# Newton and word values in PSUM, shorter steps for w_out's row blocks, products of w3 and w_out in set order

## The chip, the cores and the metric

The kernel runs on one NeuronCore of a Trainium2 chip. The metric is the device time in microseconds (us) of one execution; lower is better. Before the change the median of three runs is 1493.96 us.

The engines that matter are TensorE (PE, matrix products into PSUM), VectorE (DVE), ScalarE (ACT), GpSimd (POOL), and SyncE (SP), whose queue issues the DMA transfers here. Each engine works through its own instructions in a fixed order and waits when an operand or a buffer isn't there yet.

## The reference

```python
def _attn_ref(q, k, v, g_norm):                       # 8 batches, 8 heads, 576 rows, 64 columns
    kv = np.einsum('bhsd,bhse->bhde', k, v)
    out = np.einsum('bhsd,bhde->bhse', q, kv)
    rms = np.sqrt(np.mean(out * out, axis=-1, keepdims=True) + 1e-06)
    return (out / rms * g_norm).astype(np.float32)

def _moe_ref(x, w_in, w_out):                         # 4608 x 512, 512 x 2048, 2048 x 512
    h = x @ w_in
    g = h * np.cos(h)
    return (g @ w_out).astype(np.float32)

def _moe2_ref(x, w1, w2, w3, w_out):                  # 512 x 1024 (w1, w2), 1024 x 1024, 1024 x 512
    a = x @ w1
    b = x @ w2
    h = a * b @ w3
    return (h @ w_out).astype(np.float32)
```

The output of each is the x of the next. The weights come as float64, so the kernel gets them as pairs of 32-bit words.

## The kernel before

Products are taken in three passes over pairs of rounded values: each operand is split into hi (an ACT copy, L122) and lo (a subtraction, L124), and `three` (L863 to L866) multiplies hi by hi (L864), hi by lo (L865) and lo by hi (L866).

There are three stages. In the first, up to about 555 us, 144 steps `h_0` to `h_143` each make 128 of the 2048 columns of h for one block of 512 tokens: 12 products of 512 columns in one PSUM bank. After each, ACT and DVE make g from h (L1425, L1426, then the sine at L1399 and the product at L1400, which frees the bank), and for each four such tiles POOL makes four sums (L829 to L832) that are stored with the tiles. In among these steps, by a plan of step numbers (`at(n, where, ...)`, L1368 to L1390), attention goes on for units of 288 rows: `kv` and `out` products, the squares, the inverse root by Newton's method (`emit_newton`, 11 DVE instructions on 128x18 values), and its product with `o` on POOL. Also in among them, weights arrive in chunks of 512 columns of word pairs, whose float32 value DVE makes in four instructions (`Chunk.convert`, L153, L154, L157, L160) after ACT's absolute value at L152. A chunk whose buffer is a `g` or `stage` tile belongs to w_out (u), or comes in the next stage (d, o, a); a chunk of `i` belongs to w_in.

In the second stage, from about 530 to 880 us, g @ w_out is made as seven products of sums of blocks (`part`, tiles X, Y, V, L1027). The sums of w_out (`left_stage`, four groups kk of row blocks, stored by `left_store` and loaded again by `left_pair`) and the first two blocks of g (`load_right`, `split_right`) are made during the last steps of the first stage, from step 122 on. In the third stage w3 @ the second w_out is made first (`emit_wc`, tiles wc and wchl), so that a * b is multiplied by that one matrix; the products are X and V (L1245) and `o`.

PSUM holds eight banks: `acc0` to `acc3` in `ps_acc`, two of `ps_h`, and two of `ps_a` (tag `pa`), which the attention's small products share. A bank is taken again when its last reader is done. DVE's and ACT's instructions and the products stand in the order in which the program was written, but for stretches outside a manual schedule, which a scheduler orders. The DMA queue of SP is one line: a transfer that waits for its buffer or its source holds up all behind it.

## Time and profile before

| | us |
|---|---|
| median of three runs | 1493.96 (1492.59 to 1496.93) |
| the profiled execution | 1492.64 |
| its span | 1490.8 |
| PE busy in the span | 1448.2 (97%) |
| DVE busy | 1002.3 (67%) |
| ACT busy | 695.0 (47%) |
| POOL busy | 630.3 (42%) |
| mean granted clock of TensorE | 0.989 |

The span runs from the first to the last instruction; 1.84 us of the execution lie around it. PE's 42.6 us without work stand in a few places, each named in a table of waits by line and by what released it. [...] In the timeline a bracket gives an instruction's idle time before it and what ended that. Where an instruction of DVE is shown long, it may have stood in the engine without getting on; the time of the same instruction elsewhere tells.

### The profile page before, as it was taken

The page shows a single profiled execution, that of the slowest core. Times are in us where ns is not written, and L with a number is a line of the kernel's source. Part 1 is how long each engine was busy: PE and PEld are TensorE (multiplying, and loading weights), DVE is VectorE, ACT ScalarE, POOL GpSimd, SP SyncE. Part 2 cuts the span into 40 slices and gives each one's busy share as a digit, 9 for nine tenths or more (in the row PEclk, how much of TensorE's full clock was granted, in tenths as well). Part 3 has the DMA queues.
Part 4 walks back from the last instruction along what each step waited for, and adds up shares of the span by engine and source line. Part 5 has one row for each costly group of instructions (what it writes and reads, how often), then busy time and mean ns, then how long its engine had stood idle before and what let it go on. Part 6 is the DMA issues. An engine that isn't in the chain of part 4 may idle for free.

```text
span 1490.8 us, 21208 instructions
## 1 busy us (share of the span) xinstructions
PE 1448.2 (97%) x7632; PEld 1239.4 (83%) x7632; DVE 1002.3 (67%) x1451; ACT 695.0 (47%) x1320; POOL 630.3 (42%) x461
## 2 busy tenths in 40 slices
PE   8999999989989989999999998999999999999998
PEld 6777777777767768998888887999999898999997
DVE  4898876695797768999997338654554555544553
ACT  4656555545545536555555435433443333433331
POOL 0053853676475762222222407543544236444330
PEclk8999999999999989999999999999999999999999
DMA  9265986867777889999999762122220323223312
GB/s 354 92 224 185 327 255 189 280 227 259 235 235 267 277 309 352 376 355 352 367 363 335 243 213 94 43 85 86 71 71 29 114 72 119 92 72 127 128 65 78
DMA packets 146506, 298.75 MB, mean 200 GB/s; under 512 B 16256, under 2 KB 54240, under 8 KB 146400
## 3 DMA queue, kind: packets, MB, share of 16 engines
q1 hardware_dynamic: 145696, 296.80, 57.9%
q8 instruction: 60, 0.98, 0.3%
q10 hardware_dynamic: 704, 0.59, 0.1%
q14 instruction: 46, 0.38, 0.1%
HBM read 184.92 MB, written 112.42 MB: 199 GB/s over the span
## 4 chain that ended last, share of the span: by engine, by line
PE 80%; DVE 9%; DMA 5%; issue 3%; POOL 2%; ACT 1%; SPq 0%; POOLq 0%; DVEq 0%; ACTq 0%
PE X L1245 13%; PE X L1027 12%; PE V L1027 7%; PE V L1245 6%; PE h L864 6%; PE h L865 5%; PE h L866 5%; PE o L865 4%; PE o L864 4%; PE o L866 4%; PE Y L1245 3%; PE Y L1027 3%; PE kv L272 1%; DVE x L124 1%; DVE u L1426 1%
## 5 line engine op out<-in xcount | busy, mean ns | idle before, releaser
L864 PE MATMUL h<-x,w_in 128*128 128x512 f32 x576 | 237.9, 413 | 17.2 <-DVE u L1400 15.0
L1245 PE MATMUL X<-xc,w 128*128 128x384 f32 x1152 | 226.7, 337 | 5.3 <-DVE wchl L124 3.1
L124 POOL TENSOR_TENSOR xc<-x2r,xc 128x768 fp32r<-128x768 f32 x70 | 134.5, 1930 | 228.8 <-ACT xc L122 228.8
L865 PE MATMUL h<-x,w_in 128*128 128x512 f32 x576 | 226.6, 393 | 0.2 <-DVE x L124 0.2
L866 PE MATMUL h<-x,w_in 128*128 128x512 f32 x576 | 226.7, 394 | 0.0
L1245 PEld LDWEIGHTS X<-xc,w 128*128 128x128 f32 x1152 | 204.5, 189 | 13.0 <-DVE wchl L124 3.5
L1027 PE MATMUL X<-g_hl,wl 128*128 128x512 f32 (+1 forms) x960 | 200.2, 368 | 0.0
L1027 PEld LDWEIGHTS X<-g_hl,wl 128*128 128x128 f32 x960 | 167.7, 189 | 30.2
L122 ACT ACTIVATE g_hl<-g_raw 128x1024 fp32r<-128x1024 f32 x126 | 127.2, 1053 | 106.8 <-PE V L1027 31.5
L124 POOL TENSOR_TENSOR g_hl<-g_raw,g_hl 128x1024 fp32r<-128x1024 f32 x31 | 80.1, 2584 | 224.2 <-ACT g_hl L122 177.2
L1426 DVE SCALAR_TENSOR_TENSOR u<-h,r 128x512 f32<-128x512 f32 x136 | 93.2, 685 | 91.3 <-ACT r L1425 70.0
L864 PEld LDWEIGHTS h<-x,w_in 128*128 128x128 f32 x576 | 109.0, 189 | 48.7 <-DVE u L1400 20.1
L124 DVE TENSOR_TENSOR g_hl<-g_raw,g_hl 128x1024 fp32r<-128x1024 f32 x95 | 117.1, 1259 | 44.1 <-ACT g_hl L122 43.9
L1425 ACT ACTIVATE r<-h 128x512 int32<-128x512 f32 x136 | 81.1, 597 | 133.2 <-PE h L866 132.9
L1253 ACT ACTIVATE s<-X 128x384 f32<-128x384 f32 x144 | 66.7, 488 | 152.0 <-PE X L1245 151.9
L866 PEld LDWEIGHTS h<-x,w_in 128*128 128x128 f32 x576 | 109.2, 190 | 23.7
L865 PEld LDWEIGHTS h<-x,w_in 128*128 128x128 f32 x576 | 109.3, 190 | 23.3 <-DVE x L124 1.1
L1245 PE MATMUL V<-xc,w 128*128 128x384 f32 x576 | 116.2, 335 | 0.0
L864 PE MATMUL o<-wchl,ab 128*128 128x512 f32 x288 | 112.3, 391 | 0.7 <-DVE part L1336 0.5
L865 PE MATMUL o<-wchl,ab 128*128 128x512 f32 x288 | 113.0, 392 | 0.0
L866 PE MATMUL o<-wchl,ab 128*128 128x512 f32 x288 | 110.5, 393 | 0.0
L1399 ACT ACTIVATE u<-u 128x512 f32<-128x512 f32 x136 | 85.2, 626 | 48.4 <-DVE u L1426 47.2
(179 smaller groups left out, 2596.3 us busy)
## 6 DMA issues: line engine op xcount, KB each, us to landing
g_raw<-g SPq DMA_DIRECT2D x126, 512.0 KB
x2r<-x_all SPq DMA_DIRECT2D x44, 384.0 KB
kvraw<-in_kv_main_dram SPq DMA_DIRECT2D x32, 512.0 KB
g<-ta SPq DMA_DIRECT2D x32, 512.0 KB
g<-tb SPq DMA_DIRECT2D x32, 512.0 KB
g<-u SPq DMA_DIRECT2D x28, 512.0 KB
g<-u SPq DMA_DIRECT2D x40, 256.0 KB
part<-o SPq DMA_DIRECT2D x36, 256.0 KB
```

The costliest lines, as they stand in the source:

```text
L122: hi = nc.scalar.activation(dst[:, 0], src, AF.Copy)
L124: lo = lo_engine.tensor_tensor(dst[:, 1], src, f32(dst[:, 0]), ALU.subtract)
L272: nc.tensor.matmul(ps[d], k[:, d], v[:, d], start=fresh and i == 0, stop=i == NC, skip_group_check=True,)
L864: nc.tensor.matmul(ps, w[0], x[0], start=first, stop=False)
L865: nc.tensor.matmul(ps, w[0], x[1], start=False, stop=False)
L866: return nc.tensor.matmul(ps, w[1], x[0], start=False, stop=last).ins
L1027: nc.tensor.matmul(ps, w[:, a, i2, ws], g[:, b, q], start=first and half == 0 and q == 0 and n == 0, stop=last and final and q == KH - 1 a ...
L1245: nc.tensor.matmul(ps, w[:, self.i, a, k], x[:, b, k], start=first and k == 0 and n == 0, stop=last and k == 1 and n == 2, skip_group_chec ...
L1253: copied.append(nc.scalar.activation(s, ps, AF.Copy).ins)
L1399: nc.scalar.activation(u, u, AF.Sin, bias=HALF_PI, scale=TWO_PI)
L1425: nc.scalar.activation(r, h_ps[n], AF.Identity, bias=0.25, scale=INV_2PI)
L1426: nc.vector.scalar_tensor_tensor(u, h_ps[n], INV_2PI, r, ALU.mult, ALU.subtract)
```

## The change

Four things change. In `Chunk.convert`, word chunks with a `g` or `stage` buffer make their value in a bank of `ps_a`; the last of the four DVE instructions writes the result to SBUF, as before. In `emit_newton`, the values x and t stand in a bank of `ps_a`; y stays in SBUF. The step `h_8` takes bank `acc2` and `h_9` takes `acc3` in place of the two of `ps_h`, and unit 6 of attention starts at step 15 in place of 14. The row blocks of w_out begin every three steps from 122 in place of every four, one subtraction goes from POOL to DVE, the loads and splits of g's first blocks stand at other steps (each half of a split in a step of its own, the halves of blocks 1 and 3 on DVE in place of POOL), and the first pairs of stored sums are asked for at steps 137 and 138 in place of 142 and 143. The products of `emit_wc` stand in the order in which the program was written.

```diff
@@ -130,6 +130,7 @@
         def __init__(self, name, src, tag, put, again=False):
             self.name, self.src, self.tag, self.put = name, src, tag, put
+            self.home = "psum" if tag in ("g", "stage") else "row"
             self.again = again
         def load(self):
@@ -147,18 +148,23 @@
             lo, hi = self.words[:, :, 0], self.words[:, :, 1]
-            self.f = row(f"{self.name}_f")
-            b = self.f.bitcast(I32)
-            yield nc.scalar.activation(self.f, hi.bitcast(F32), AF.Abs)
-            yield nc.vector.tensor_scalar(self.f, self.f, MOST, LEAST, ALU.min, ALU.max)
+            if self.home == "psum":
+                f = ps_a.tile([P, CHUNK], F32, tag="pa", name=f"{self.name}_ps")
+            else:
+                f = self.f = row(f"{self.name}_f")
+            b = f.bitcast(I32)
+            yield nc.scalar.activation(f, hi.bitcast(F32), AF.Abs)
+            yield nc.vector.tensor_scalar(f, f, MOST, LEAST, ALU.min, ALU.max)
             yield nc.vector.tensor_scalar(
                 b, b, 3, 0x3FFFFFF8, ALU.logical_shift_left, ALU.bitwise_and
             )
             yield nc.vector.scalar_tensor_tensor(
                 b, hi, -0x40000000, b, ALU.bitwise_and, ALU.bitwise_or
             )
+            if self.home == "psum":
+                self.f = row(f"{self.name}_f")
             yield nc.vector.scalar_tensor_tensor(
-                b, lo, 29, b, ALU.logical_shift_right, ALU.bitwise_or
+                self.f.bitcast(I32), lo, 29, b, ALU.logical_shift_right, ALU.bitwise_or
             )
     chunks = []
@@ -329,12 +335,11 @@
     def emit_newton(u):
-        x = rs[u]
-        y, t = (
-            ap.tile([P, RS], F32, tag=f"rs{i}", bufs=2, name=f"rs{i}_{u}") for i in range(2)
-        )
+        at = ps_a.tile([P, 512], F32, tag="pa", name=f"newton_{u}")
+        x, t = (at[:, RS * i:RS * i + RS] for i in range(2))
+        y = ap.tile([P, RS], F32, tag="rs0", bufs=2, name=f"rs0_{u}")
         load["vector"] += 1000
-        nc.vector.tensor_scalar(x, x, EPS, HUGE, ALU.add, ALU.min)
+        nc.vector.tensor_scalar(x, rs[u], EPS, HUGE, ALU.add, ALU.min)
         newton(x, y, t)
         rs[u] = y
@@ -869,10 +874,11 @@
         t, m = steps[n]
         if tag:
             ps = ps_acc.tile([P, 512], F32, tag=tag, name=f"h_{n}")
-        elif n <= HM or n % 4 < 2:
+        elif n < HM or n % 4 < 2 and n > HM + 1:
             ps = ps_h.tile([P, 512], F32, tag="h", name=f"h_{n}")
         else:
-            ps = ps_acc.tile([P, 512], F32, tag=f"acc{n % 4 - 2}", name=f"h_{n}")
+            k = n % 4 - 2 if n > HM + 1 else n - HM + 2
+            ps = ps_acc.tile([P, 512], F32, tag=f"acc{k}", name=f"h_{n}")
         w, x = w_in[m], x_hl[t]
         for c in range(KD):
             h_last[n] = three(
@@ -933,7 +939,7 @@
             (vec if kk < 2 else pool).tensor_tensor(a22, a21, a22, ADD)
             left(0, kk, a11)
         if stage == 1:
-            (pool if kk else vec).tensor_tensor(a21, a11, a21, SUB)
+            (pool if kk > 1 else vec).tensor_tensor(a21, a11, a21, SUB)
             left(1, kk, a12)
         if stage == 2:
             vec.tensor_tensor(a11, a22, a11, SUB)
@@ -993,13 +999,16 @@
             nc.sync.dma_start(out=t, in_=gd[k, 2 * half + r][:, slot])
             raws[i, r] = t
-    def split_right(i):
+    def split_right(i, which=(0, 1)):
         k, p, half, _ = parts_of[i]
         W, KR, KH = shape_of(k)
-        t = x_home((0, 2, 1)[i % 3], [P, 2, KH, W], F32R, f"g_hl_{i}")
-        for r in range(2):
-            split(t[:, :, KR * r:KR * r + KR], raws.pop((i, r)), pool if r and i % 2 else vec)
-        rights[i] = t
+        if i not in rights:
+            rights[i] = x_home((0, 2, 1)[i % 3], [P, 2, KH, W], F32R, f"g_hl_{i}")
+        for r in which:
+            split(
+                rights[i][:, :, KR * r:KR * r + KR], raws.pop((i, r)),
+                pool if r and i % 2 and i > 4 else vec,
+            )
     def part(i):
@@ -1345,7 +1354,7 @@
         }
         end_of = {t: max(n for n, s in enumerate(steps) if s[0] == t) for t in range(NB)}
         ready = plan_first(HM - 1)
-        starts = (14, 22, 29, 36, 44, 52, 59, 78, 86, 93)
+        starts = (15, 22, 29, 36, 44, 52, 59, 78, 86, 93)
         for u, n in zip(range(6, NU), starts):
             ready[u] = plan_unit(u, n, u in (6, 9, 10, 11, 12, 13))
         LIGHT = (*range(48, 54), *range(64, 72), *range(80, 88), *range(98, 104), *range(114, 120))
@@ -1372,20 +1381,20 @@
         for k, n in enumerate(words):
             plan_words(n_first + k, n)
         for kk in range(4):
-            n = 122 + 4 * kk
+            n = 122 + 3 * kk
             at((117, 120, 121, 127)[kk], "end", left_load, kk)
             for k in range(4):
                 at(n + k, "mid", left_stage, kk, k)
-            for l, k in ((3, 2), (5, 3), (6, 5)):
+            for l, k in ((3, 2), (5, 3), (6, 6 if kk == 1 else 5)):
                 at(n + k, "top", left_store, kk, l)
         at(131, "end", load_right, 0)
-        at(135, "end", load_right, 1)
-        at(138, "mid", split_right, 0)
-        at(138, "end", load_right, 2)
-        at(140, "mid", split_right, 1)
-        at(140, "end", load_right, 3)
-        at(NS - 2, "end", left_pair, 0)
-        at(NS - 1, "end", left_pair, 1)
+        at(133, "end", load_right, 1)
+        at(135, "end", load_right, 2)
+        at(139, "end", load_right, 3)
+        for i in range(2):
+            for r in range(2):
+                at(134 + 2 * i + r, "mid", split_right, i, (r,))
+            at(137 + i, "end", left_pair, i)
         for i in range(len(LATE_LEFT)):
             at(NS + i, "mid", left_late, i)
@@ -1523,7 +1532,8 @@
         x0 = xc_early(0, vec)
         next(x0)
         for k, step in enumerate(wc_steps):
-            emit_wc(*step)
+            with tc.manual_schedule(engines={mybir.EngineType.PE}):
+                emit_wc(*step)
             if k + 6 < len(wc_steps):
                 load_w3(k + 6)
             if k + 2 < len(wc_steps):
```

On SP's queue, near the end of the first stage, this stood before. `w_left_3`, `w_left_5` and `w_left_6` are the stored sums of w_out, `g_raw_0` to `g_raw_3` the first four blocks of g for the second stage (two transfers each), `g_4_2` the place in memory of the last tokens' sums, and `w_pair` a pair of stored sums that comes back.

```order
L993 DMA g_raw_1_0_5147<-g_0_2_1592 128x1024
L993 DMA g_raw_1_1_5149<-g_0_3_1737 128x1024
L950 DMA w_left_3_4831<-w_out_13_4948 128x2x256
L950 DMA w_left_5_4861<-w_out_03_4945 128x2x256
L993 DMA g_raw_2_0_5226<-g_0_0_950 128x1024
L993 DMA g_raw_2_1_5228<-g_0_1_1125 128x1024
L950 DMA w_left_6_4919<-w_out_13_4948 128x2x256
L835 DMA g_4_2_5214<-u_7_4_5166 128x2x512
L836 DMA g_4_2_5214<-u_8_4_4968 128x512
L840 DMA g_4_2_5214<-ta_4_4_5215 128x2x512
L840 DMA g_4_2_5214<-tb_4_4_5216 128x2x512
L993 DMA g_raw_3_0_5283<-g_0_2_1592 128x1024
```

And now:

```order
L999 DMA g_raw_1_0_5128<-g_0_2_1584 128x1024
L999 DMA g_raw_1_1_5130<-g_0_3_1736 128x1024
L956 DMA w_left_5_4877<-w_out_03_4963 128x2x256
L999 DMA g_raw_2_0_5179<-g_0_0_950 128x1024
L999 DMA g_raw_2_1_5181<-g_0_1_1119 128x1024
L956 DMA w_left_6_4939<-w_out_13_4966 128x2x256
L972 DMA w_pair_30_5226<-w_left_3_4847 128x1024
L972 DMA w_pair_31_5254<-w_left_3_4847 128x1024
L840 DMA g_4_2_5247<-u_7_4_5198 128x2x512
L841 DMA g_4_2_5247<-u_8_4_4986 128x512
L999 DMA g_raw_3_0_5276<-g_0_2_1584 128x1024
L999 DMA g_raw_3_1_5278<-g_0_3_1736 128x1024
```

The last part of `w_left_3` has moved ahead of `g_raw_1`, out of this piece, and `w_pair_30` and `w_pair_31`, which stood behind the two sets of four transfers of `g_4_2` (rows 355 and 358 of SP's order), now stand ahead of them.

On PE, the products of the ninth step of `emit_wc` (`w3hl_1_0` is the first part of w3 for the second half, `wo2_0` a row block of the second w_out, each with hi and lo; `wc_1_0` to `wc_1_3` are four banks) stood so before:

```order
L864 MATMUL wc_1_0_8502<-wo2_0_7938,w3hl_1_0_8455 128x512
L865 MATMUL wc_1_0_8502<-wo2_0_7938,w3hl_1_0_8455 128x512
L864 MATMUL wc_1_1_8506<-wo2_0_7938,w3hl_1_0_8455 128x512
L865 MATMUL wc_1_1_8506<-wo2_0_7938,w3hl_1_0_8455 128x512
L864 MATMUL wc_1_2_8510<-wo2_0_7938,w3hl_1_0_8455 128x512
L865 MATMUL wc_1_2_8510<-wo2_0_7938,w3hl_1_0_8455 128x512
L864 MATMUL wc_1_3_8514<-wo2_0_7938,w3hl_1_0_8455 128x512
L865 MATMUL wc_1_3_8514<-wo2_0_7938,w3hl_1_0_8455 128x512
L866 MATMUL wc_1_0_8502<-wo2_0_7938,w3hl_1_0_8455 128x512
```

And now:

```order
L869 MATMUL wc_1_0_8584<-wo2_0_7994,w3hl_1_0_8532 128x512
L870 MATMUL wc_1_0_8584<-wo2_0_7994,w3hl_1_0_8532 128x512
L871 MATMUL wc_1_0_8584<-wo2_0_7994,w3hl_1_0_8532 128x512
L869 MATMUL wc_1_1_8588<-wo2_0_7994,w3hl_1_0_8532 128x512
L870 MATMUL wc_1_1_8588<-wo2_0_7994,w3hl_1_0_8532 128x512
L871 MATMUL wc_1_1_8588<-wo2_0_7994,w3hl_1_0_8532 128x512
L869 MATMUL wc_1_2_8592<-wo2_0_7994,w3hl_1_0_8532 128x512
```

The product that needs the lo part of `w3hl_1_0`, lo by hi, was the ninth of the twelve (L866) and is now the third (L871).

On ACT, the first copies of the finished wc (`wchl`, which the first X product of the third stage is held for) stood so before, among copies of w1 and w2 (`w12`) that wait for POOL:

```order
L122 ACTIVATE w3hl_1_0_8455<-w3raw_8_8357 128x512
L122 ACTIVATE xc_0_1_8458<-x2r_0_8288 128x768
L122 ACTIVATE w12_00_5_8280<-w12raw_01_8285 128x256
L122 ACTIVATE w12_01_0_8689<-w12raw_10_8696 128x256
L122 ACTIVATE w12_01_1_8690<-w12raw_10_8696 128x256
L122 ACTIVATE w12_00_6_8281<-w12raw_00_8282 128x256
L122 ACTIVATE wchl_0_8480<-wc_0_0_8293 128x512
L122 ACTIVATE wchl_1_8483<-wc_0_1_8297 128x512
```

And now:

```order
L122 ACTIVATE w3hl_1_0_8532<-w3raw_8_8422 128x512
L122 ACTIVATE xc_0_1_8535<-x2r_0_8344 128x768
L122 ACTIVATE w12_00_5_8336<-w12raw_01_8341 128x256
L122 ACTIVATE wchl_0_8559<-wc_0_0_8351 128x512
L122 ACTIVATE w12_01_0_8793<-w12raw_10_8800 128x256
L122 ACTIVATE w12_01_1_8794<-w12raw_10_8800 128x256
L122 ACTIVATE wchl_1_8562<-wc_0_1_8355 128x512
L122 ACTIVATE w12_00_6_8337<-w12raw_00_8338 128x256
```

`wchl_0` now stands ahead of the three copies of `w12` that it stood behind, and `wchl_1` ahead of the last of them, `w12_00_6`.

## Rows read from the trace of the kernel before

**Rows 1.** TensorE's waits by line and releaser: us in total, times, longest.

```profile
PE h L864 <- DVE u L1400: 15.0, 8, 4.2
...
PE X L1245 <- DVE wchl L124: 3.1, 1, 3.1
...
PE Y L1027 <- DVE g_hl L124: 2.7, 1, 2.7
...
PE h L864 <- DVE u_first L625: 2.1, 1, 2.1
...
PE Y L1027 <- POOL g_hl L124: 1.7, 1, 1.7
...
PE wc L864 <- ACT w3hl L122: 1.5, 1, 1.5
...
PE kv L272 <- ACT o L683: 1.2, 1, 1.2
```

**Rows 2.** TensorE's timeline, three stops: start, us, line, operation, [idle before <- releaser].

```profile
287.55 0.69 PE L272 MATMUL kv<-kvraw 128*64 128x64 f32 x16 [1.40 <-DMA kvraw<-in_kv_main_dram]
...
326.91 0.50 PE L864 MATMUL h<-x,w_in 128*128 128x512 f32 x1 [4.18 <-DVE u L1400]
...
524.61 0.50 PE L864 MATMUL h<-x,w_in 128*128 128x512 f32 x1 [2.90 <-DVE u L1400]
```

**Rows 3.** Stretches: length, busy us (count) from PE to POOL, PEclk, DMA share.

```profile
80.00:125.00 45.00, 43.84 (x293) 33.41 (x293) 44.55 (x59) 29.06 (x72) 24.95 (x16) 1.00 0.75 251
...
325.00:330.00 5.00, 3.09 (x9) 2.48 (x10) 4.90 (x10) 2.42 (x6) 1.62 (x3) 0.80 0.62 228
...
400.00:440.00 40.00, 35.56 (x154) 27.90 (x153) 37.13 (x65) 20.11 (x44) 25.37 (x21) 0.96 0.55 178
...
560.00:880.00 320.00, 320.00 (x1571) 271.90 (x1570) 251.73 (x286) 166.07 (x209) 81.05 (x33) 1.00 0.93 332
```

**Rows 4.** DVE's timeline, two Newton passes: 316.50 to 325.64, 405.19 to 407.84.

```profile
316.50 0.98 DVE L337 TENSOR_SCALAR rsx<-rsx 128x18 f32<-128x18 f32 x1
...
317.73 1.16 DVE L325 TENSOR_TENSOR rs<-rsx,rs 128x18 f32<-128x18 f32 x1
...
325.46 0.18 DVE L327 SCALAR_TENSOR_TENSOR rs<-rs,rs 128x18 f32<-128x18 f32 x1
...
405.19 0.53 DVE L337 TENSOR_SCALAR rsx<-rsx 128x18 f32<-128x18 f32 x1
...
407.66 0.18 DVE L327 SCALAR_TENSOR_TENSOR rs<-rs,rs 128x18 f32<-128x18 f32 x1
```

**Rows 5.** POOL's timeline beside the first of these passes.

```profile
317.53 1.32 POOL L830 TENSOR_TENSOR ta<-u,ta 128x512 f32<-128x512 f32 x1
```

**Rows 6.** DVE's groups by line and shape: count, busy, mean ns, idle before.

```profile
L1400 DVE TENSOR_TENSOR u<-u,h 128x512 f32<-128x512 f32 x136 | 91.9, 676 | 0.1
...
L160 DVE SCALAR_TENSOR_TENSOR u_f<-u_w,u_f 128x512 int32<-128x512 int32 x16 | 18.4, 1152 | 0.6
...
L153 DVE TENSOR_SCALAR u_f<-u_f 128x512 f32<-128x512 f32 x16 | 6.9, 428 | 0.0
...
L455 DVE TENSOR_SCALAR rs_first<-ms_first 96x48 f32<-96x48 f32 x1 | 0.2, 197 | 0.0
```

**Rows 7.** SP's and DVE's timelines near 517: a store, and who waits for it.

```profile
517.46 0.47 SPq L835 DMA_DIRECT2D g<-u  x1
...
523.27 0.69 DVE L1426 SCALAR_TENSOR_TENSOR u<-h,r 128x512 f32<-128x512 f32 x1 [5.50 <-DMA g<-u]
```

**Rows 8.** ACT's timeline: the late pair of stored sums.

```profile
543.53 1.15 ACT L122 ACTIVATE wl<-w_pair 128x512 fp32r<-128x512 f32 x2 [10.55 <-DMA w_pair<-w_left]
```

**Rows 9.** DVE's and ACT's timelines before the first X product.

```profile
906.23 1.22 DVE L124 TENSOR_TENSOR w3hl<-w3raw,w3hl 128x512 fp32r<-128x512 f32 x1
...
911.04 1.27 DVE L124 TENSOR_TENSOR wchl<-wc,wchl 128x512 fp32r<-128x512 f32 x2
...
909.79 2.04 ACT L122 ACTIVATE wchl<-wc 128x512 fp32r<-128x512 f32 x4
```

## The prediction

> **What bounds the kernel now.** I read the page first: PE is busy for 1448.2 of 1490.8 us, so the end can move only by PE's waits (42.6 us), by the time that PE runs at half clock behind them, or by a wait that is added. The table of PE's waits by releaser comes second [rows 1]. Most of it is h waiting for DVE's last product of a step, which frees the bank: 15.0 us in 8 places. Beside it the reader is to see single stops: 3.1 us before the first X product of the third stage, 2.7 and 1.7 us before two Y products, 2.1 us for `u_first`, 1.5 us in wc, 1.2 us for ACT. Third, PE's timeline gives the places: 4.18 us at 326.91 and 2.90 at 524.61 [rows 2]; of the other 7.9 us of the eight, 7.1 lie in four stops between 427 and 450, 0.25 at 275.6 and 0.63 at 491.3. At 287.55 `kv` waited 1.40 us for its data [rows 2].
>
> A long stop has a second price. The granted clock is 0.80 in the 5 us that hold the end of the stop at 326.91, and PE makes 9 products in 3.09 busy us [rows 3], 0.34 us each, where a step of h at full clock has 0.227 (12 in 2.72). Nine products lose (0.34 − 0.227) x 9 = 1.0 us, and the next stretch about half of that: I take 1.5 us for each stop near 3 us or longer (327, 436, 525, 550, 912).
>
> Fourth, what DVE did before those stops. The Newton pass that ends just before 326.91 takes from 316.50 to 325.64, 9.1 us for 11 instructions on 18 columns; the pass at 405.19 takes 2.65 us for the same 11 [rows 4]. The short instruction lasts 0.18 us; the long ones last 1.0 to 1.2, and they end with the instruction that POOL has running, 1.3 us each [rows 5]. POOL had no such chain at 405. So it isn't the arithmetic: a DVE instruction whose operands are all in SBUF stands while POOL works on SBUF. The products at L1400, with one operand in PSUM, average 0.676 us over 136 [rows 6], in the same stretches, with nothing near 1.3 added. That is the profile's best evidence for the change.
>
> **The change part by part.** The sum is made against the profiled execution, 1492.64 us, 1.32 below the median of the runs; a saving is then taken from the median.
>
> Banks of `h_8` and `h_9`. `h_9` stopped 2.1 us for the tile that `u_first` frees [rows 1]. With `acc3` it is held by step 6 in place of 7, done one step earlier, so the stop goes. What is late next is DVE: it is busy 44.55 of the 45 us from 80 on [rows 3], so a PE that is 2.1 us early meets DVE later. The stop of 1.2 us for ACT at 110.3 has one more step of slack with unit 6 a step later. Together at most 3.3; at least about 1.2, what DVE idled just ahead. I take 2.5, as most of DVE's work there follows h and moves up with it.
>
> Newton in PSUM. Each pass still has 11 instructions. The kind isn't in the trace with these operands. Nearest row: 96x48 from PSUM takes 0.197 us [rows 6] against 0.18 for 128x18 in SBUF. So 11 x 0.21 (with issue) to 11 x 0.25, 2.3 to 2.8 us a pass; the other end is no escape, 9.1 as now. I take 2.5, by the L1400 row. Before 326.91 that is 9.1 − 2.5 = 6.6 us less ahead of a stop of 4.18, which is covered; the 0.25 at 275.6 too. The pass ahead of 287.55 lasted 8.4 us, and behind its result on SP's queue stands the store that held up the `kv` data; 1.40 goes if the transfer moves up with it. Sum: 0.25 + 1.40 + 4.18 + 1.5 of clock = 7.3. At the other end, nothing.
>
> [...]
>
> Words in PSUM. The four instructions (L153, L154, L157, L160) for the 16 u chunks have means from 0.428 [rows 6] over 0.905 and 0.898 to 1.152 us [rows 6], 3.38 in all. In PSUM the first two lose a fast form (0.43 for 512 columns): their price isn't in the trace; at best 0.43, at worst 0.68, the time of a product with an operand in PSUM [rows 6]. I take 0.68, so 4 x 0.69 = 2.8 us, 0.6 less than now. Where POOL is idle the word costs 0.5 more (2.8 against 2.24); in the second stage that lies beside PE, as DVE is busy 252 of 320 us and PE never waits [rows 3].
>
> From 400 to 440 DVE is busy 37.13 of 40 us [rows 3], and PE's four stops up to 450 are DVE's lag. There lie one slow Newton pass (6.1 us; 3.6 less) and four words (14.2 us; 3.1 less): 6.7 us against 7.1 us of stops and 1.5 of clock. I take 7; bounds 4.5 (the words gain nothing) and 8.6.
>
> End of the first stage. The stop at 524.61 follows from a queue: DVE stood 5.50 us at 523.27 for u's tile, whose store SP issued at 517.46 [rows 7], since it stood behind the load of `g_raw_2`, which waited for a split. `g_raw_2` is asked for three steps earlier now, and so is its split. The two Y stops come from `g_hl_3`, split behind sums that ACT got 10.55 us late [rows 8], as `w_pair` was asked for behind g's stores, and behind POOL's last chain; both reasons go (`w_pair` is ahead on SP, the split on DVE at step 137). What stands to be saved: 0.63 + 2.90 + 2.7 + 1.7 + two times 1.5 of clock = 10.9. Against that, `w_pair` now waits on SP for stores to land, with g's stores queued behind it and u's tiles behind these; and four row blocks in 13 steps instead of 17 put about 30 us of DVE's splits into 35 us. I charge 1.5 for new stops there, and 0.5 for one bank: `ms_7` (near 173 us) now gets the bank of `kv_4_1` a step after it, where it had three. Net 9; bounds 5 and 11.
>
> wc. Lo by hi is now the third product. In the ninth step, which ran from 905.44, DVE's lo is done only at 907.45 [rows 9]; the third product would start at 905.9, so PE stops 1.5 us there. Then `wchl_0`: ACT made it at 909.79 [rows 9], 0.4 us after the copies that waited for POOL, and DVE's half came at 911.04 [rows 9], which ended the 3.1 us. Now both stand earlier, so X starts at about 909.8 + 0.4 instead of 911.77; with the clock I take 1.5 saved, bounds 3 saved and 2 lost.
>
> Sum: 2.5 + 7.3 + 7 + 9 + 1.5 = 27.3. 1492.64 − 27.3 = 1465.3; on the scale of the median 1493.96 − 27.3 = 1466.7, say **1467 us**.
>
> **The rivals.** Nearly every stop that is touched goes: 2.1 + 1.2 + 5.8 + 7.1 + 0.6 + 2.9 + 4.4 + 4.6 = 28.7 and 5 x 1.5 of clock = 36.2, so 1458. For it speaks that each has a cause that is taken away; against it that DVE is full near 80 to 125 and 400 to 450, so a stop is only pushed on.
>
> PSUM doesn't spare these instructions the wait for POOL (y in SBUF and the words themselves remain operands). Then Newton and words give nothing, and 2.5 + 9 + 1.5 = 13 remain: 1481. Against it: L1400 has the same mix of operands.
>
> The gain is given back in the second stage, by transfers: DMA engines are busy 0.93 of 560 to 880 [rows 3], that leaves 22 us of them. If the loads came no earlier, only wc and a little of the end would remain, about 3 us: 1491. Against it: PE never waits there, and the loads are asked for by PE's own progress.
>
> Slower: DVE at steps 122 to 134. Four row blocks (I estimate 7.6 us each: three splits and two sums beside POOL), 16 pairs of L1426 and L1400 at 1.3 us and four half splits of about 2.3 us make 60 us in 16 steps, 43.5 us. If all of it fell so, DVE would lag 16 us, PE would stop for it with about five half clock stretches (8), and the other parts' 17 us wouldn't pay for that: 24 − 17 = 7, so 1501. It decides once DVE lags by more than the two steps (5.4 us) that h's four banks allow. For it: 60 us is more than the stretch holds, and DVE already stood full for the 45 us from 80 on [rows 3] with stops of PE beside it. Against it: the splits have places that shift by a step at no price as long as the lag is under that, and two halves on POOL took longer than they will on DVE.
>
> **How the numbers follow.** My forecast has 0.58 (1460 to 1475), nearly all stops gone 0.14, PSUM no escape or other losses of that size 0.16, given back 0.05, slower 0.07. The range reaches from the second case to the third, 1457 to 1482, and leaves out the last two. A difference of 0.3% is 4.5 us, about the least that a measurement tells from none. Faster holds the first three and a little of the fourth, 0.89; the same 0.04; slower 0.07.
>
> **What would show it.** Right: Newton's 11 instructions at 0.18 to 0.25 us beside POOL's sums; words' four near 0.68 each; no stop of PE at 327, 436, 525 and 550, with the clock at 1.00 there; X starting sooner after wc's last product than 3 us. Wrong: long Newton rows with an operand in PSUM; DVE at 5.0 of each 5 us from 460 to 510 with PE's stops beside it; PE waiting for a load between 560 and 880; a stop at `ms_7` of more than 1.5 us; more than 2 us in the ninth step of wc.

## The result, and the profile after

The changed kernel takes 1476.2 us (median of four, 1472.5 to 1480.3) against 1493.3 us before: a ratio of 0.988 with a 95% interval of 0.985 to 0.991. So it is faster by 17.1 us; I had said 27. The profiled execution is the slowest of the four, 1480.28 us with a span of 1478.4, 12.4 us under the span before.

Three views of the changed kernel show what became of the stops of [rows 1]. First PE's waits (in total, times, longest): h for DVE is down from 15.0 to 11.3 us only, in 10 places, and X waits for ACT in the second stage, which it didn't before. The third stage's first X product (898.61) doesn't wait any more; 0.4 us in place of 3.1 are left, before its second tile (900.19). `u_first`, `kv` and the two Y stops are gone from the table.

```profile
PE h L869 <- DVE u L1409: 11.3, 10, 2.9
...
PE X L1036 <- ACT s L1055: 2.1, 1, 2.1
...
PE X L1254 <- DVE wchl L124: 0.4, 1, 0.4
```

PE's timeline gives the places of the largest, and one of four small ones near 100:

```profile
99.37 0.50 PE L869 MATMUL h<-x,w_in 128*128 128x512 f32 x1 [0.72 <-DVE u L1409]
...
488.87 0.50 PE L869 MATMUL h<-x,w_in 128*128 128x512 f32 x1 [2.88 <-DVE u L1409]
...
517.18 0.50 PE L869 MATMUL h<-x,w_in 128*128 128x512 f32 x1 [1.90 <-DVE u L1409]
...
577.35 1.99 PE L1036 MATMUL X<-g_hl,wl 128*128 128x512 f32 x6 [2.07 <-ACT s L1055]
```

Only the one at 517.18 stands where one stood before, and is the old one of 524.61, smaller. At 327 [rows 2] nothing is left, of the 7.1 us between 427 and 450 two stops of 1.16 and 0.73 are. New ones have come at step 15 (99.37), steps 129 and 130 (1.38 and 0.46 us), step 134 (488.87) and on an X product of the second stage (577.35).

The groups of DVE's instructions answer to [rows 4, 6]:

```profile
L157 DVE TENSOR_SCALAR u_ps<-u_ps 128x512 f32<-128x512 f32 x16 | 11.1, 691 | 0.0
...
L166 DVE SCALAR_TENSOR_TENSOR u_f<-u_w,u_ps 128x512 int32<-128x512 int32 x16 | 11.0, 687 | 0.6
...
L332 DVE SCALAR_TENSOR_TENSOR newton<-newton,rs 128x18 f32<-128x18 f32 x36 | 6.6, 184 | 1.3
...
L327 DVE TENSOR_SCALAR rs<-newton 128x18 int32<-128x18 int32 x12 | 2.1, 177 | 0.4
...
L342 DVE TENSOR_SCALAR newton<-rsx 128x18 f32<-128x18 f32 x12 | 2.0, 171 | 0.0
```

Newton's instructions average 0.17 to 0.18 us, a pass has 1.98 us of work (23.7 over twelve, 47.7 before), and the word's four take 0.69 to 0.70 each, 2.77 in all. The longest of the 132 Newton instructions takes 0.185 us in each of the nine kernels below and here that have them in PSUM, and 1.24 to 1.27 in each of the five that don't.

Executions differ by where h begins: `h_0` starts at 36.41 us in the profile before, at 39.01 in this one, and from 33.4 to 42.1 in those below, with the same instructions ahead of it (the granted clock, a share of full speed, is 0.50 to 0.58 from 20 to 35 in one and 0.50 to 0.55 from 25 to 35 in the other; b2_relief and d1_prefetch6 below show no such stretch up to 45, and have the latest `h_0` and the earliest). So I compare starts counted from `h_0`. The table gives, for the start of a step of h and for one X product of the third stage that waits 0.86 us for ACT in every run (at 1189.10 before, at 1176.70 after), how much earlier (−) it is than before.

| kernel | step 10 | 36 | 92 | 120 | 136 | X |
|---|---|---|---|---|---|---|
| the changed kernel | −2.4 | 0.3 | −7.8 | −15.2 | −9.0 | −15.0 |
| a1_newton | 0.0 | −0.3 | 1.1 | −2.3 | −2.3 | −1.9 |
| a2_words | 0.0 | −0.3 | −5.1 | −7.7 | −7.8 | −6.1 |
| a3_banks | −2.4 | 0.3 | −0.5 | −0.4 | −0.4 | −0.4 |
| a4_blocks | 0.0 | 0.5 | 1.5 | 1.6 | 7.7 | −1.0 |
| a5_wc | 0.1 | 0.3 | 0.1 | 0.3 | 0.1 | 0.7 |
| c1_noblocks | −2.5 | 0.1 | −8.0 | −15.9 | −16.2 | −18.5 |
| b2_relief | −2.4 | 0.2 | −7.9 | −14.6 | −8.6 | −17.0 |
| b3_four | −2.6 | 0.1 | −8.0 | −16.0 | −17.2 | −23.5 |
| d1_prefetch6 | −2.4 | 0.3 | −7.8 | −14.7 | −15.8 | −22.1 |
| d2_latepairs | −2.5 | 0.2 | −7.9 | −15.3 | −16.4 | −26.5 |
| d3_oldbanks | 1.2 | 1.1 | −7.0 | −14.8 | −16.0 | −20.7 |
| e1_words_behind | −2.4 | 0.2 | −7.9 | −15.3 | −16.4 | −24.2 |

One profile each. What that is worth, seven of them tell: the changed kernel, c1, b2, b3, d1, d2 and e1 have the same instructions in the same order on every engine up to step 120, and differ among themselves by 0.3 us at steps 10 to 92 and by 1.4 us at step 120. Smaller differences are no finding. The first row says it all: 2.4 us won by step 10 and lost by step 36; 8 more won by step 92 and 7 by step 120; 6 lost by step 136; and 6 won from there to X.

In the windows, the 45 us from 80 on still hold 44.11 us of DVE's work ([rows 3]: 44.55); from 400 to 440 PE is busy 38.11 in place of 35.56; and a stretch at 0.68 of the clock stands behind the new stop at 488.87:

```profile
80.00:125.00 45.00, 42.19 (x274) 30.64 (x275) 44.11 (x59) 29.32 (x69) 24.94 (x16) 1.00 0.73 237
...
400.00:440.00 40.00, 38.11 (x171) 30.18 (x170) 37.10 (x75) 20.61 (x45) 29.44 (x27) 1.00 0.76 252
...
490.00:495.00 5.00, 5.00 (x17) 3.95 (x16) 5.00 (x8) 2.65 (x6) 2.35 (x2) 0.68 0.94 225
```

### The profile page after: what moved, and what is told of

It reads as the page before. It is cut to its first block, busy times and chain, and to the rows that moved or that the text cites. A ratio compares the mean times of both kernels' runs of the same rounds, so it can differ in the third digit from the quotient of the medians.

```text
span 1478.4 us, 21176 instructions
## 1 busy us (share of the span) xinstructions
PE 1449.3 (98%) x7632; PEld 1238.4 (84%) x7632; DVE 958.3 (65%) x1454; ACT 693.7 (47%) x1320; POOL 613.9 (42%) x458
## 4 chain that ended last, share of the span: by engine, by line
PE 84%; DVE 8%; DMA 3%; issue 2%; POOL 2%; ACT 1%; SPq 0%; DVEq 0%; POOLq 0%; ACTq 0%
PE X L1254 13%; PE X L1036 12%; PE h L869 7%; PE h L870 7%; PE h L871 7%; PE V L1254 6%; PE V L1036 6%; PE o L870 4%; PE o L869 4%; PE o L871 4%; PE Y L1254 3%; PE Y L1036 3%; PE kv L278 2%; PE out L679 1%; DVE u L1409 1%
## 5 line engine op out<-in xcount | busy, mean ns | idle before, releaser
L869 PE MATMUL h<-x,w_in 128*128 128x512 f32 x576 | 236.2, 410 | 11.3 <-DVE u L1409 11.3
L124 POOL TENSOR_TENSOR xc<-x2r,xc 128x768 fp32r<-128x768 f32 x70 | 134.1, 1926 | 229.4 <-ACT xc L122 224.9
L871 PE MATMUL h<-x,w_in 128*128 128x512 f32 x576 | 225.4, 391 | 0.0
L124 POOL TENSOR_TENSOR g_hl<-g_raw,g_hl 128x1024 fp32r<-128x1024 f32 x29 | 75.1, 2591 | 225.4 <-ACT g_hl L122 184.7
L124 DVE TENSOR_TENSOR g_hl<-g_raw,g_hl 128x1024 fp32r<-128x1024 f32 x97 | 120.5, 1269 | 60.1 <-ACT g_hl L122 60.0
L869 PEld LDWEIGHTS h<-x,w_in 128*128 128x128 f32 x576 | 108.5, 188 | 43.5 <-DVE u L1409 16.8
L871 PEld LDWEIGHTS h<-x,w_in 128*128 128x128 f32 x576 | 108.6, 189 | 23.5
L871 PE MATMUL o<-wchl,ab 128*128 128x512 f32 x288 | 110.7, 393 | 0.0
L1254 PEld LDWEIGHTS V<-xc,w 128*128 128x128 f32 x576 | 102.0, 188 | 2.6 <-POOL w L124 0.4
```

The source lines that it names most:

```text
L124: lo = lo_engine.tensor_tensor(dst[:, 1], src, f32(dst[:, 0]), ALU.subtract)
L869: nc.tensor.matmul(ps, w[0], x[0], start=first, stop=False)
L871: return nc.tensor.matmul(ps, w[1], x[0], start=False, stop=last).ins
L1254: nc.tensor.matmul(ps, w[:, self.i, a, k], x[:, b, k], start=first and k == 0 and n == 0, stop=last and k == 1 and n == 2, skip_group_chec ...
```

## The experiments

Five kernels make one part of the change alone on the kernel before. Each diff shows only the lines that tell the edit.

**Newton alone** (a1_newton): of the diff, `emit_newton` only.

```diff
+        at = ps_a.tile([P, 512], F32, tag="pa", name=f"newton_{u}")
+        x, t = (at[:, RS * i:RS * i + RS] for i in range(2))
```

> The kernel before with Newton's x and t in PSUM and nothing else. My theory: a DVE instruction with one operand in PSUM does not stand while POOL works, so each pass takes 2.3 to 2.8 us and PE's stops at 287.6 (1.40) and 326.9 (4.18 with about 1.7 of half clock) go, 7 to 8 us by step 82; between 427 and 450 the slow pass gives 3.6 us more, so 10 to 12 us by step 120. Rival: the short passes only bring DVE to its next full stretch sooner, and the stops of 427 to 450 keep their 7 us: 7 to 8 us by step 120.

Measured: 1489.7 us, ratio 0.9945 (0.9925 to 0.9965). By the profile 6.0 us are won between steps 80 and 82, but 5.7 are lost again by step 88: PE stops 3.0 us at 346.62, and the clock is 0.59 in the 5 us from 345. Timeline of that kernel:

```profile
340.62 3.10 POOL L358 TENSOR_TENSOR o<-o,bc 128x288 f32<-128x288 f32 x4
...
341.47 0.31 ACT L122 ACTIVATE x<-o 128x128 fp32r<-128x128 f32 x1 [4.87 <-POOL o L358]
...
345.28 0.69 DVE L1425 SCALAR_TENSOR_TENSOR u<-h,r 128x512 f32<-128x512 f32 x1 [7.56 <-ACT r L1424]
...
346.62 0.80 PE L863 MATMUL h<-x,w_in 128*128 128x512 f32 x1 [3.00 <-DVE u L1399]
```

DVE has nothing to do for 7.56 us: it waits for ACT, ACT for POOL's product with the norms, which stands behind g's sums and splits of x. So my theory held for the pass and fell for its worth, 2.3 us by step 120: neither I nor the rival had this stop. In the changed kernel, with the words short too, it doesn't come.

**Words alone** (a2_words): of the diff, `Chunk` only.

```diff
+            self.home = "psum" if tag in ("g", "stage") else "row"
+                f = ps_a.tile([P, CHUNK], F32, tag="pa", name=f"{self.name}_ps")
```

> The kernel before with the words' value in PSUM and nothing else. My theory: four instructions of about 0.69 us each whatever POOL does, so the four words of 400 to 450 give about 3 us of the 7 us of stops there, and nothing changes before step 110: 3 us in all. Rival: the first two lose their fast form (0.43 to 0.69 us), which takes back what the wait for POOL cost: no change at step 120, and at the end within 2 us.

Measured: 1488.1 us, ratio 0.9935 (0.991 to 0.9959). Both were wrong: 7.7 us by step 120, of which 5 lie between steps 36 and 92 already, as the stop before 326.9 shrank to 2.36 with Newton's pass untouched. I had counted words only where PE stopped, between 400 and 450.

**Banks alone** (a3_banks): `HM` bounds in `emit_h`, and the start of unit 6.

```diff
-        starts = (14, 22, 29, 36, 44, 52, 59, 78, 86, 93)
+        starts = (15, 22, 29, 36, 44, 52, 59, 78, 86, 93)
```

> The kernel before with other banks for h of steps 8 and 9 and unit 6 a step later. My theory after the changed kernel's trace: h_10 starts 2.4 us earlier, but DVE is full from 80 to 165, so PE stops for DVE between steps 14 and 34 and by step 36 nothing is left (within 0.6 us). Rival, my prediction: 2.5 us are kept at step 36 when the other edits are away, and what the changed kernel lost there belongs to another edit.

Measured: 1493.25 us, ratio 0.9978 (0.996 to 0.9996). As the theory has it: 2.4 us at step 10, nothing at step 36. The timed runs are some 3 us faster, by an interval that ends just under 1, and the profile shows only 0.4 of it at X; where the rest would come from is open. The window of 80 to 125 shows DVE as full as before:

```profile
80.00:125.00 45.00, 42.29 (x267) 30.81 (x266) 44.56 (x60) 28.71 (x70) 24.93 (x16) 1.00 0.75 252
```

**Row blocks alone** (a4_blocks): `left_stage`, `split_right` and the plan's numbers.

```diff
-            n = 122 + 4 * kk
+            n = 122 + 3 * kk
```

> The kernel before with w_out's row blocks, loads and splits at their new steps and nothing else. My theory after the changed kernel's trace: POOL, still at g's sums when three of w_out's sums come behind them, holds DVE for some 5 us near step 134, which costs PE 4 to 6 us up to step 136, and the stops at 524.6, 548.9 and 552.8 (7.4 us with 3.5 of half clock) shrink by about 9: 3 to 5 us better in all. Rival, my prediction: the denser blocks cost 1.5 us and 9 us are gained; second rival: dense blocks lose more than the late stops give, and it is slower by 1 to 4 us.

Measured: 1494.5 us, ratio 0.9993 (0.9975 to 1.0011), no difference that the runs can tell. The trace has both halves: 6.2 us lost between steps 120 and 136, 8.7 won from there to X. The stop at step 134 is there without any other part of the change, and the last one of h too:

```profile
501.70 0.50 PE L864 MATMUL h<-x,w_in 128*128 128x512 f32 x1 [2.90 <-DVE u L1403]
...
530.11 0.79 PE L864 MATMUL h<-x,w_in 128*128 128x512 f32 x1 [2.04 <-DVE u L1403]
```

That leaves 2.5 us, of which 0.9 is the clock in wc (see the next run), so my 3 to 5 us in all was too much; the rival of 9 us is out, and the second rival, 1 to 4 us slower, isn't borne out.

**Order of wc alone** (a5_wc):

```diff
+            with tc.manual_schedule(engines={mybir.EngineType.PE}):
+                emit_wc(*step)
```

> The kernel before with wc's products in the order written and nothing else. My theory: the stop of 3.07 us before the first X product falls to about 0.4, and wc's third products wait for DVE's lo parts by 0.2 to 1.5 us in all: 1 to 3 us better, half clock included. Rival: what is saved before X is lost in wc, no change (within 0.5 us) from the first wc product to the third X tile.

Measured: 1497.4 us, ratio 0.9994 (0.9974 to 1.0014). The first X product now starts 7.3 us after the stop in wc (904.26 to 911.58); before it was 9.2 (902.58 to 911.77). What follows waits instead: wc's third products 0.22 and 0.95 us, and the second X tile 0.72 for the split of wchl.

```profile
904.26 0.50 PE L864 MATMUL wc<-wo,w3hl 128*128 128x512 f32 x1 [1.32 <-ACT w3hl L122]
...
909.16 0.50 PE L866 MATMUL wc<-wo,w3hl 128*128 128x512 f32 x1 [0.95 <-DVE w3hl L124]
...
911.58 1.22 PE L1245 MATMUL X<-xc,w 128*128 128x384 f32 x6
913.52 1.31 PE L1245 MATMUL X<-xc,w 128*128 128x384 f32 x6 [0.72 <-DVE wchl L124]
```

From the stop in wc to the third X tile are 17.0 us (18.7 before), to the mark at X 285.7 (286.5). By these two profiles that is a gain of 1.7 and then 0.8 us, which would speak for my theory's 1 to 3. But the difference is a stretch of the clock: before, it is 0.66 from 910 to 915, behind X's stop. In a3 and a4, which have the old order and X's stops of 3.09 and 1.84 us, it is 1.00 there, and they need 17.3 and 285.6 us. So at the mark the order itself is worth nothing, as the rival says. The stretch stands in three of the five profiles with the old order (286.5 to 287.6 us to the mark) and in none of the nine with the new one (285.7 to 285.8), so keeping it away may be the order's doing. The 0.7 in the table's last column arose ahead of wc.

**The changed kernel without the row blocks** (c1_noblocks): all of the diff but a4's part.

> The changed kernel with w_out's row blocks, loads and splits at their old steps. My theory: Newton and the words together give more than the sum of their runs alone (2.3 and 7.7 us by step 120), since with one of them left slow DVE only carries its lag to the next stretch: 15 us by step 120, kept to step 142, and the three late stops (2.9, 2.7, 1.7 us with half clock) stay as before, so 14 to 16 us better than the kernel before in all. Rival: the row blocks at their new steps are what makes the sum larger than its parts, and without them it is 10 us.

Measured: 1478.4 us, ratio 0.9868 (0.9826 to 0.9911). By step 120 it has 15.9 us where the three parts alone add up to 2.3 + 7.7 + 0.4 = 10.4. That fits the theory that with Newton or the words still slow DVE and POOL bring the lag to the next full stretch. The rival is out: the sum is there without the row blocks. The late stops are back, two of the three here (the third is 0.98 in place of 1.73):

```profile
509.08 0.50 PE L869 MATMUL h<-x,w_in 128*128 128x512 f32 x1 [3.01 <-DVE u L1406]
...
533.53 2.93 PE L1033 MATMUL Y<-g_hl,wl 128*128 128x512 f32 x6 [2.65 <-DVE g_hl L124]
```

In all it is 18 us faster than the kernel before, more than my 14 to 16. At X it is 3.5 us ahead of the changed kernel in the profiles; the timed runs don't tell the two apart. So no gain of the row blocks' part of the change shows here.

**POOL relieved** (b2_relief). In the changed kernel's timeline DVE stands 5.08 us before group 2's difference, since three of w_out's instructions follow four sums of g on POOL:

```profile
479.96 1.84 POOL L836 TENSOR_TENSOR tb<-u 128x512 f32<-128x512 f32 x1
...
481.76 1.30 POOL L837 TENSOR_TENSOR tb<-u,ta 128x512 f32<-128x512 f32 x1
...
483.00 1.30 POOL L947 TENSOR_TENSOR w_out<-w_out,w_out 128x512 f32<-128x512 f32 x1
...
484.24 1.30 POOL L939 TENSOR_TENSOR w_out<-w_out,w_out 128x512 f32<-128x512 f32 x1
...
485.63 1.27 POOL L942 TENSOR_TENSOR w_out<-w_out 128x512 f32<-128x512 f32 x1
...
486.93 0.69 DVE L945 TENSOR_TENSOR w_out<-w_out,w_out 128x512 f32<-128x512 f32 x1 [5.08 <-POOL w_out L942]
```

So in this kernel three of them go to DVE:

```diff
-            (vec if kk < 2 else pool).tensor_tensor(a22, a21, a22, ADD)
+            (vec if kk < 3 else pool).tensor_tensor(a22, a21, a22, ADD)
-            (pool if kk > 1 else vec).tensor_tensor(a21, a11, a21, SUB)
+            (pool if kk > 2 else vec).tensor_tensor(a21, a11, a21, SUB)
-            (pool if kk else vec).tensor_tensor(a12, a12, a11, SUB)
+            (pool if kk > 1 else vec).tensor_tensor(a12, a12, a11, SUB)
```

> The changed kernel with three of w_out's sums and differences (group 2's first two, group 1's last) on DVE in place of POOL. My theory: the stop of 2.9 us with half clock at step 134 comes from DVE waiting 5.1 us for POOL, whose line of g's sums stands ahead of these; it goes, 3 to 4.5 us better than the changed kernel. Rival: DVE itself is full there, and three more instructions of 0.7 to 1.8 us put the stop elsewhere: no better.

Measured: 1478.0 us, ratio 0.9864 (0.9823 to 0.9905); 8.6 us at step 136 in place of 9.0. My theory fell, the rival holds: three DVE instructions (one of them moved here, two splits) with all operands in SBUF, 1.8 us each beside POOL, stand between two of DVE's h products, and PE stops for the same 2.9 us, at step 132 in place of 134. The two stops of steps 129 and 130 are as in the changed kernel.

```profile
480.66 1.78 DVE L124 TENSOR_TENSOR wl<-w_out,wl 128x512 fp32r<-128x512 f32 x1
...
482.36 1.77 DVE L939 TENSOR_TENSOR w_out<-w_out,w_out 128x512 f32<-128x512 f32 x1
...
484.05 1.75 DVE L124 TENSOR_TENSOR wl<-w_out,wl 128x512 fp32r<-128x512 f32 x1
...
485.72 0.68 DVE L1435 SCALAR_TENSOR_TENSOR u<-h,r 128x512 f32<-128x512 f32 x1
...
487.05 0.79 PE L869 MATMUL h<-x,w_in 128*128 128x512 f32 x1 [2.89 <-DVE u L1409]
```

**A row block every four steps** (b3_four), the rest of the change kept:

```diff
-            n = 122 + 3 * kk
+            n = 122 + 4 * kk
-            for l, k in ((3, 2), (5, 3), (6, 6 if kk == 1 else 5)):
+            for l, k in ((3, 2), (5, 3), (6, 5)):
-        at(133, "end", load_right, 1)
+        at(135, "end", load_right, 1)
-                at(134 + 2 * i + r, "mid", split_right, i, (r,))
-            at(137 + i, "end", left_pair, i)
+                at(134 + 3 * i + r, "mid", split_right, i, (r,))
+            at(140 + i, "end", left_pair, i)
```

> The changed kernel with a row block every four steps again; g's first loads and splits stay at or near their new steps (the split of block 1 at steps 137 and 138, the first stored pairs asked for at 140 and 141). My theory: the stops of steps 130 to 134 (6 us with the clock) come from the blocks' closeness alone and go, while the early loads and splits still remove the stops before the Y products: 5 to 7 us better than the changed kernel. Rival: the gain at the Y products needs the early stored pairs, which come at 140 and 141 here, and the stops return: 0 to 2 us better.

Measured: 1470.4 us, ratio 0.9814 (0.9776 to 0.9851), some 8 us under c1 and b2 on the same chip. At X it is 8.5 us ahead of the changed kernel in the profiles, more than my 5 to 7; the rival is out. The stops of steps 129 to 134 and that at 517.18 are gone, and no Y stop is above 0.4. The edit moves more than the blocks, but the first split of g stands behind `h_134` in the order, so the stops up to step 134 can't come from the splits. What is left is X (a row of SP with x2 spans two issues):

```profile
563.41 5.21 SPq L999 DMA_DIRECT2D g_raw<-g  x2
...
564.73 1.06 ACT L122 ACTIVATE g_hl<-g_raw 128x1024 fp32r<-128x1024 f32 x1 [2.78 <-DMA g_raw<-g]
...
565.99 0.63 ACT L156 ACTIVATE d_ps<-d_w 128x512 f32<-128x512 f32 x1 [0.20 <-DMA d_w<-in_w12w_dram]
...
567.19 2.08 PE L1036 MATMUL X<-g_hl,wl 128*128 128x512 f32 x4 [2.87 <-ACT s L1055]
```

**A word load earlier** (d1_prefetch6), on b3:

```diff
-            if 7 <= i:
-                prefetch(min(state["conv"] + (1 if i == 7 else 2), len(chunks)))
+            if 6 <= i:
+                prefetch(min(state["conv"] + (1 if i < 8 else 2), len(chunks)))
```

> The version with a row block every four steps, and the first load of word pairs of the second stage asked for one part of the seven-product scheme earlier. My theory: X waits 2.87 us for ACT there since ACT's next instruction in line is the absolute value of words whose load stood on SP's queue behind loads of g that waited for their buffers; asked for earlier it is there, and the stop goes with its half clock: 3 to 5 us better than the version with four steps. Rival: DMA is full there and the earlier load only delays g's, whose split becomes the next stop: within 1 us of it.

Measured: 1467.2 us, ratio 0.9824 (0.9782 to 0.9866), the same as b3. The rival's number holds: X still stops 1.96 us, and ACT waits 1.57 for g's load. Its reason isn't shown: ACT waited for that load in b3 too (2.78), and the DMA share is 0.82 from 560 to 565. The four issues that stretch over 6.16 us on SP wait for their buffers: each leaves within 0.03 us of the end of a split of g (L124, on DVE or POOL), here as in b3.

```profile
556.77 6.16 SPq L999 DMA_DIRECT2D g_raw<-g  x4
...
562.06 1.06 ACT L122 ACTIVATE g_hl<-g_raw 128x1024 fp32r<-128x1024 f32 x1 [1.57 <-DMA g_raw<-g]
...
565.67 2.58 PE L1036 MATMUL X<-g_hl,wl 128*128 128x512 f32 x7 [1.96 <-ACT s L1055]
```

**Stored pairs late** (d2_latepairs), on b3:

```diff
-            at(140 + i, "end", left_pair, i)
+            at(NS - 2 + i, "end", left_pair, i)
```

> The version with a row block every four steps, and the first pairs of stored sums asked for at the last two steps again (142 and 143 in place of 140 and 141). My theory: the Y stops (2.7 and 1.7 us before) came from the late pairs as much as from the late splits: with the pairs late again behind g's stores, 2 to 4 us of stops with half clock return before the Y products. Rival: the early splits on DVE alone remove them: within 1 us of the version with four steps.

Measured: 1466.4 us, ratio 0.9815 (0.9786 to 0.9844). The rival holds: no Y stop above 0.57 comes back, so the earlier loads and splits, all on DVE, remove them, not the early pairs.

```profile
527.37 1.88 PE L1036 MATMUL Y<-g_hl,wl 128*128 128x512 f32 x7 [0.57 <-DVE g_hl L124]
```

**Old banks** (d3_oldbanks), on b3: `emit_h` and the start of unit 6 as before the change.

> The version with a row block every four steps, with the old banks of h_8 and h_9 and unit 6 at step 14. My theory: DVE is full from 80 to 165, so the banks are worth nothing by step 36: the stops of 2.1 and 1.2 us return and the four of 0.5 to 0.8 go, within 0.7 us at step 36. Rival, as I predicted for the banks: 2.5 us worse at step 36 and at the end.

Measured: 1474.3 us, ratio 0.9863 (0.9836 to 0.989), beside 0.9824 for d1 and 0.9815 for d2 on the same chip. The two old stops are back and the four small ones gone. At step 36 it is 1.0 us behind b3, but it lost 1.7 at steps 10 and 11, to a stretch at 0.71 of the clock behind the first stop that none of the other kernels with this stop has. At step 120 its −14.8 lies among the −14.6 to −16.0 of the same steps with the new banks. So the profiles show no gain of the banks in h's time, as the theory has it. The timed runs speak otherwise: 7 to 8 us between it and d1 or d2. That stays open; against d2, which also asks for its pairs later, `h_0` is 1.9 us later in its profile, and X's stop is 2.93 here, 1.72 there.

```profile
78.03 0.50 PE L869 MATMUL h<-x,w_in 128*128 128x512 f32 x1 [2.14 <-DVE u_first L630]
...
80.00:85.00 5.00, 5.00 (x17) 3.97 (x16) 4.05 (x8) 2.71 (x5) 0.67 (x1) 0.71 0.05 17
...
113.88 0.69 PE L278 MATMUL kv<-kvraw 128*64 128x64 f32 x16 [0.87 <-ACT o L688]
```

**Words behind the part** (e1_words_behind), on d2: `convert` and `prefetch` after `part(i)`.

```diff
+            part(i)
             if 9 <= i and state["conv"] < state["load"]:
                 convert(1)
             if 7 <= i:
                 prefetch(min(state["conv"] + (1 if i == 7 else 2), len(chunks)))
-            part(i)
```

> The version with four steps and late pairs, and in the second stage the words' first instruction written behind each part's products and copies in place of ahead of them, so that ACT's copy of X (s) stands ahead of the absolute value that waits for its words. My theory: X's stop of 1.72 us at that copy goes, 1.5 to 3 us better than the version with late pairs. Rival: g's own load, for whose split ACT waits 2.7 us just ahead of that copy, is as late, and the stop only shrinks: within 1 us.

Measured: 1468.7 us, ratio 0.981 (0.9783 to 0.9836), as d2. The rival holds again: the words are out of ACT's way, and it stands 3.34 us for g's data just before the copy that X waits for.

```profile
566.09 1.06 ACT L122 ACTIVATE g_hl<-g_raw 128x1024 fp32r<-128x1024 f32 x1 [3.34 <-DMA g_raw<-g]
...
567.06 1.06 ACT L1055 ACTIVATE s<-X 128x512 f32<-128x512 f32 x2
...
567.69 1.65 PE L1036 MATMUL X<-g_hl,wl 128*128 128x512 f32 x6 [2.90 <-ACT s L1055]
```

## Why the prediction was right and wrong

**The mechanism** held: in these kernels a DVE instruction with one operand in PSUM doesn't stand while POOL works (at most 0.185 us for Newton's and 0.70 for the words', whatever POOL does). Newton's instructions take about the same time there as in SBUF: 0.177 us for 18 columns from PSUM to SBUF, 0.184 with operands in PSUM and SBUF and the result in PSUM, against 0.18 before with all in SBUF [rows 4] where they don't stand. The word's first instruction takes longer, as I had said: 0.691 us in PSUM, 0.428 in SBUF before [rows 6].

**Newton**, 7.3 us to step 92: 8.1 in the changed kernel (0.3 to −7.8). But it isn't Newton's alone: alone it keeps nothing there, the words alone keep 4.8. The step that failed here is the pairing of each edit with the stop next to it: the two are worth what they are together.

**400 to 450**, 7 us: 7.3. Right, and the shares too: from step 92 to 120 Newton alone gives 3.4 us and the words alone 2.6, where I had 3.6 and 3.1.

**Banks**, 2.5 us kept: the step that failed is "as most of DVE's work there follows h and moves up with it". 2.4 us came at step 10 and were gone at step 36, as PE met a DVE that is full from 80 on, in four stops of 0.6 to 0.8. The view that says so was in the prediction ([rows 3], 44.55 of 45); I let it take a little off the gain, and it took all of it. By the profiles the lower bound should have been 0; the timed runs of a3 and d3 give the banks more, by a way that no profile here shows. No stop came at `ms_7`, for which I had charged 0.5.

**End of the first stage**, 9 us: the step that failed is "I charge 1.5 for new stops there". The old stops went as said (the two Y stops whole, 524.61 from 2.90 to 1.90), but the denser blocks cost 6.1 us from step 120 to 136 in the changed kernel and 6.2 alone; the mechanism of my slower rival took place at a quarter of its size. Part of it I had not seen: at step 134 it is POOL that holds DVE, and when POOL is relieved DVE itself is late, at step 132 (b2). My sign of being wrong, DVE at 5.0 of each 5 us with PE's stops beside it, came from 455 to 480 only; from 480 to 490 DVE stands for POOL. The wait behind `w_pair` that I had named came too: g's stores left SP at 508.71, behind it, and DVE stood 6.71 us for them. With the pairs at 140 and 141 (b3) g's stores of 499 leave ahead of the first pair (503.16), and PE doesn't stop there, though DVE still stands 5.35 us for a store of tb (at 510.52).

```profile
507.82 0.79 SPq L972 DMA_DIRECT2D w_pair<-w_left  x2
...
508.71 0.38 SPq L840 DMA_DIRECT2D g<-u  x1
...
515.84 0.69 DVE L1435 SCALAR_TENSOR_TENSOR u<-h,r 128x512 f32<-128x512 f32 x1 [6.71 <-DMA g<-u]
```

Then X's 2.07 us with a stretch at 0.85 and 0.81 of the clock (575 to 585). A like stop of 1.19 us, at 591.81, stands in a3, so the row blocks aren't needed for one. Here the rival on transfers has its part: in the changed kernel ACT waits for g's load, then for the words', and then makes the copy that X is held for.

```profile
574.89 1.06 ACT L122 ACTIVATE g_hl<-g_raw 128x1024 fp32r<-128x1024 f32 x1 [1.15 <-DMA g_raw<-g]
...
576.15 0.63 ACT L156 ACTIVATE d_ps<-d_w 128x512 f32<-128x512 f32 x1 [0.20 <-DMA d_w<-in_w12w_dram]
...
576.72 1.06 ACT L1055 ACTIVATE s<-X 128x512 f32<-128x512 f32 x2
```

By d1 and e1 this stop hangs on g's load more than on the words: either of the words' delays can be taken away, and ACT then stands for g. Each of these transfers leaves SP within 0.05 us of the end of a split of g, which frees its buffer, in the changed kernel, b3, d1, d2 and e1 alike, so at least part of its delay comes from the splits; what makes those late when h is early was not tried.

**wc**, 1.5 us: 0.8 from the stop in wc to the mark at X (a5 and the changed kernel), all of it the stretch of the clock behind X, which a3 and a4 lack with the old order. The step that failed is taking an earlier first X for an earlier end: the second tile waits in its place.

So the sum 27.3 was made of 16.8 up to step 120, measured 15.2, and 10.5 after it, measured −0.2; the version with four steps has 7.5 there. That version differs by a few numbers of the plan, and beats both kernels: 0.981 of the time before, in three builds of it (b3, d2, e1). The 1476.2 us lie within my range of 1457 to 1482, but outside the 1460 to 1475 of the forecast. The range's upper end was worked out for the case that PSUM is no escape, which is not what happened; other losses of that size shared its chance without a working. That the losses at the end of the first stage stayed within it was in part luck.

## What to carry to other kernels

Taking away a stop of PE won nothing here where DVE, which it waits for, had no idle time behind it: the banks' 2.4 us of step 10 were gone by step 36, with DVE busy 44.11 of the 45 us from 80. So count the helper's work from the stop to its next idle stretch, not the stop. Edits that shorten two links of one chain are priced together, since one alone may only move the lag on, as Newton's did (6.0 us won by step 82, 5.7 of them lost by step 88). Before work is packed denser on a plan, take from the order what stands ahead of it on each engine, POOL's line too: in the changed kernel DVE stood 5.08 us for it.

## What was not expected of the hardware

POOL's own sums vary too: a 128x512 sum takes 1.84 us at 479.96, with a DVE instruction on SBUF alone beside it (a split, 0.68 us at 479.97), and 1.30 at 481.76, where DVE mostly has nothing to do; beside Newton's long instructions before, one took 1.32 [rows 5]. So by these rows POOL may be held too; no run takes that by itself. A split of the same shape takes 1.78 us in b2's timeline, beside POOL. Of the time up to `h_0`, 8.6 us (33.4 to 42.1) differ between executions with the same instructions there, about half of what the change brought.
